# Decay rates without a logarithm, weights staged in idle buffer slots, and the order and engines of all work as one list

## The chip, the cores and the metric

One core of a Trainium2 chip runs the whole program. The time is the device time of one execution in microseconds (us), and the median of several executions is quoted. The profile covers one execution; its span, from the first to the last instruction, is 1.8 us shorter than the time of the same execution (1.77 to 1.88 in the thirteen profiled runs whose time is on record). TensorE does the matmuls, VectorE and ScalarE work on vectors (ScalarE has the table functions), GpSimd does simple vector work, and SyncE issues transfers.

## The reference, cut to what matters

```python
# 4 x 5824 tokens, 256 channels
log_a = 8 * sigmoid(r_gate) * log(clip(sigmoid(a_param)))   # decay per token and channel
a_t   = exp(log_a)
x_g   = sqrt(max(1 - a_t * a_t, 1e-6)) * sigmoid(i_gate) * x
h     = a_t[:, t] * h + x_g[:, t]        # a recurrence over the 5824 tokens
# then, token by token, with w1, w2 (256 x 1024), w3 (1024 x 1024), w_out (1024 x 256)
out   = ((h @ w1) * (h @ w2)) @ w3 @ w_out
```

The kernel computes w3 @ w_out once, at the start (the "fold"), so that each token needs two up products and one down product.

## The kernel before

The 23296 tokens are 46 chunks: one of 256 and 45 of 512. For each chunk c: load r, i and x; tanh of r and i on ScalarE; turn to channel-major, on TensorE for the first chunks and by a transfer for the rest; decay (an exp on ScalarE, scaled by the decay rate `la4`); square, root, gate, scan; cast of the state to bf16 (y); up products `pa` and `pb` in four parts mp; copy of `pa` from PSUM (the memory that TensorE writes to) to SBUF (the working memory) as `sa`; product `g_t = sa * pb` on VectorE; down product `po`; eviction; store. What the argument touches:

```python
def rates():                                   # from a_param to the decay rate
    nc.scalar.activation(out=la4, in_=la4, func=AF.Exp, scale=-1.0)
    nc.scalar.activation(out=la4, in_=la4, func=AF.Ln, bias=1.0)
    nc.vector.tensor_scalar(la4, la4, -1.0, LN_LO, op0=ALU.mult, op1=ALU.max)
    nc.vector.tensor_scalar(la4, la4, LN_HI, 4.0, op0=ALU.min, op1=ALU.mult)

def load_w(key, piece):                        # 14 weight pieces of 512 KB
    T[key] = held.tile([P, NCB, CT], F32, name="wf", tag="wf", bufs=NWF)   # NWF = 2
    nc.sync.dma_start(out=..., in_=piece)      # cut

def copy(c, mp):
    sa = ffn.tile([P, 2, CT], BF16, name="sa", tag="sa")
    copy_to((c, mp) in DV_COPY, sa[:, :, :w], T["pa", c, mp][:, :, :w])    # VectorE or ScalarE

def product(c, mp):
    nc.vector.tensor_mul(out=T["g", c][...], in0=T["sa", c, mp][...], in1=T["pb", c, mp][...])   # cut

DV_COPY = {(0, 1)}; DV_EVAC = {9}; DV_SQUARE = {2, 3, 10, 13}
W_CAST = {"w1": "POOL", "w2": "POOL", "wo": "POOL", "w3": "POOL"}
# ... a list scheduler with due times, offsets per kind of work and 470 single moves
#     works out the order of all instructions when the kernel is built (cut)
```

In these traces each engine runs its own instructions in the order of the program. That matters for everything below: a late operand or a long instruction holds up all that stands behind it on the same engine (at 368 to 378 us, shown below, a copy stands behind six pieces of scans and TensorE waits 1.26 us for it).

## Time and profile before

| | before |
|---|---|
| median of 3 runs | 528.69 us (525.78 to 528.93) |
| span of the profiled run | 526.2 us |
| TensorE, VectorE, ScalarE, GpSimd busy | 498.7, 433.9, 456.0, 342.6 us |
| first up product, first down product | 23.58, 64.32 us |
| decay rates ready | 10.45 us |

To read the start I use one number throughout, the **TensorE time lost** at a point: the time at which a down product starts, less the useful matmul time that stands before it in TensorE's program (each matmul at its undisturbed spacing, the warm-up matmuls at nothing). It only uses start times, and it shows where time is lost: where the number rises. The prediction reads the same thing by hand. Before the change it is 28.1 us at the first down product, of which 21.4 lie before the first up product, and 32.7 at the last: 4.6 are lost in the long middle. Two lines of the stretches (window, length, then busy us and count of TensorE, weight loads, VectorE, ScalarE, GpSimd, then granted clock, DMA share, GB/s) stand for that middle:

```profile
100.00:200.00 100.00, 97.72 (x610) 58.70 (x609) 89.70 (x76) 90.36 (x108) 68.30 (x52) 1.00 1.09 285
...
300.00:400.00 100.00, 100.00 (x619) 60.36 (x617) 87.39 (x70) 94.17 (x111) 75.74 (x57) 1.00 0.97 254
```

From 100 to 400 us (the stretch in between is in the prediction) VectorE has 10 to 14 us free in each 100, ScalarE 5 to 10. And TensorE's timeline (start, duration, engine, line, operation, tiles, count) dates the first down product:

```profile
64.32 1.91 PE L399 MATMUL po<-wp_sb,g_t 128*128 128x256 bf16 x16
```

### The profile page before, as it was taken

Reading aid. Unit: us, or ns where it says so; the run is one execution under the profiler, and the core shown is the slowest. Engines: PE = TensorE matmul, PEld = TensorE weight load, DVE = VectorE, ACT = ScalarE, POOL = GpSimd, SP = SyncE. Lnnn points to the kernel's source line nnn. Section 1 sums busy time; section 2 is a strip of 40 time slices with the busy share of each in tenths; the row PEclk is TensorE's granted clock in tenths of the full one; section 3 lists DMA queues with packets and bytes.
Section 4 is the critical chain, followed back from the end, with each engine's and each line's share of the span. In section 5 each row is a group of like instructions: output and inputs, shape, how many; then the busy total and the mean of one; then the engine's idle time right before and its main releaser. Section 6 shows DMA issues by size and latency. Waiting matters only on the chain.

```text
span 526.2 us, 8784 instructions
## 1 busy us (share of the span) xinstructions
PE 498.7 (95%) x3204; PEld 306.8 (58%) x3204; DVE 433.9 (82%) x376; ACT 456.0 (87%) x535; POOL 342.6 (65%) x270
## 2 busy tenths in 40 slices
PE   1589999999999999999999999999999999999997
PEld 0456666655555656555566565565665665656555
DVE  1799788998899979987888889898878988698842
ACT  5999898999898889989989989998999998965453
POOL 3478966785828768855886968878587667392100
PEclk9999999999999999999999999999999999999999
DMA  8989999999999998988897999968999875533113
GB/s 302 395 279 338 268 262 274 296 295 236 278 320 243 266 322 189 265 220 222 223 257 216 258 331 253 264 195 222 277 232 271 239 185 157 161 83 87 53 40 102
DMA packets 174604, 123.28 MB, mean 234 GB/s; under 512 B 84448, under 2 KB 170208, under 8 KB 174560
## 3 DMA queue, kind: packets, MB, share of 16 engines
q1 hardware_dynamic: 174288, 122.71, 84.9%
q8 instruction: 25, 0.41, 0.3%
q14 instruction: 19, 0.16, 0.1%
q10 hardware_dynamic: 272, 0.00, 0.0%
HBM read 78.91 MB, written 23.86 MB: 195 GB/s over the span
## 4 chain that ended last, share of the span: by engine, by line
PE 79%; DMA 9%; ACT 3%; DVE 3%; POOL 3%; issue 2%; SPq 0%; ACTq 0%; DVEq 0%; POOLq 0%
PE po L399 27%; PE pa L368 26%; PE pb L368 25%; DMA wf<-in_moe_w_dram 5%; DMA wf<-in_moe_w_out_dram 1%; ACT sa L376 1%; DVE h_t L349 1%; DVE g_t L388 1%; DMA rt<-th_r 1%; POOL w_t L436 1%; DMA r_t<-in_r_gate_dram 1%; POOL w_sb L436 1%; PE ptr L286 1%; PE pw L464 0%; POOL wo_sb L436 0%
## 5 line engine op out<-in xcount | busy, mean ns | idle before, releaser
L388 DVE TENSOR_TENSOR g_t<-sa,pb 128x1024 bf16<-128x1024 bf16 (+1 forms) x184 | 219.7, 1201 | 64.0 <-ACT sa L376 44.6
L368 PEld LDWEIGHTS <-w_sb 128*128 128x128 bf16 x1472 | 143.6, 98 | 141.9 <-issue 5.5
L376 ACT CAST sa<-pa 128x1024 bf16<-128x1024 f32 (+1 forms) x183 | 181.7, 1002 | 36.0 <-PE pa L368 35.1
L368 PE MATMUL pb<-y_t,w_sb 128*128 128x512 bf16 (+1 forms) x736 | 186.8, 377 | 1.3 <-DVE g_t L388 0.6
L368 PE MATMUL pa<-y_t,w_sb 128*128 128x512 bf16 (+1 forms) x736 | 186.4, 377 | 1.6 <-DVE g_t L388 1.3
L399 PE MATMUL po<-wp_sb,g_t 128*128 128x256 bf16 x1456 | 181.5, 273 | 0.0
L399 PEld LDWEIGHTS <-g_t 128*128 128x128 bf16 x1456 | 142.4, 98 | 45.9
L349 DVE TENSOR_TENSOR_SCAN h_t<-a_t,h_t,nrm 128x512 f32<-128x512 f32 (+3 forms) x90 | 132.0, 1481 | 0.7
L278 POOL TENSOR_TENSOR u_t<-th_i,x_t 128x512 bf16<-128x512 f32 x78 | 113.9, 1476 | 2.1 <-DMA x_t<-in_x_dram 1.7
L314 POOL TENSOR_TENSOR nrm<-a_t 128x512 f32<-128x512 f32 (+1 forms) x84 | 100.7, 1213 | 10.8 <-ACT a_t L307 9.5
L357 POOL CAST y_t<-h_t 128x1024 bf16<-128x1024 f32 x40 | 50.6, 1265 | 80.7 <-DVE h_t L349 75.1
L262 POOL TENSOR_SCALAR th_i<-th_i 128x1024 f32<-128x1024 f32 x42 | 54.5, 1300 | 41.0 <-ACT th_i L257 40.9
L376 ACT COPY ot<-po 128x512 f32<-128x512 f32 (+1 forms) x89 | 51.6, 583 | 16.9 <-PE po L399 16.8
L307 ACT ACTIVATE a_t<-rt,la 128x512 f32<-128x512 bf16 x74 | 58.7, 819 | 3.2 <-DMA rt<-th_r 1.8
L334 DVE SCALAR_TENSOR_TENSOR nrm<-nrm,ut 128x1024 f32<-128x1024 f32 x39 | 52.9, 1358 | 0.3 <-DMA ut<-u_t 0.2
L257 ACT ACTIVATE th_i<-i_t 128x1024 f32<-128x1024 f32 (+1 forms) x46 | 48.3, 1053 | 0.6 <-POOL u_t L278 0.5
L323 ACT ACTIVATE nrm<-nrm 128x1024 f32<-128x1024 f32 (+1 forms) x46 | 47.6, 1056 | 0.2
L250 ACT ACTIVATE th_r<-r_t 128x1024 bf16<-128x1024 f32 x37 | 39.1, 1061 | 2.0 <-DMA r_t<-in_r_gate_dram 1.7
L286 PE MATMUL ptr<-ident,th_r 128*128 128x128 bf16 x68 | 6.1, 246 | 14.9 <-ACT th_r L248 7.6
L323 ACT ACT_TABLE_LOAD x14 | 18.0, 1283 | 0.3
L307 ACT ACTIVATE a_t<-ptr,la 128x512 f32<-128x512 bf16 (+1 forms) x18 | 12.8, 751 | 2.8 <-PE ptr L286 1.4
L286 PEld LDWEIGHTS <-th_r 128*128 128x128 bf16 x68 | 5.1, 110 | 16.5 <-ACT th_r L248 14.3
(40 smaller groups left out, 142.3 us busy)
## 6 DMA issues: line engine op xcount, KB each, us to landing
r_t<-in_r_gate_dram SPq DMA_DIRECT2D x45, 512.0 KB, 6.2
i_t<-in_i_gate_dram SPq DMA_DIRECT2D x45, 512.0 KB, 5.4
x_t<-in_x_dram SPq DMA_DIRECT2D x45, 512.0 KB, 5.0
out_dram<-ot SPq DMA_DIRECT2D x89, 256.0 KB, 3.9
wf<-in_moe_w_dram SPq DMA_DIRECT2D x12, 512.0 KB, 5.6
wf<-in_moe_w_out_dram SPq DMA_DIRECT2D x2, 512.0 KB, 7.4
ut<-u_t SPq DMA_TRANSPOSE x39, 4.7
rt<-th_r SPq DMA_TRANSPOSE x37, 5.4
```

The source lines that it names most:

```text
L262: nc.gpsimd.tensor_scalar(t, t, 1.0, 1.0, op0=ALU.add, op1=ALU.mult)
L278: nc.gpsimd.tensor_mul(out=u.rearrange("p cb j q -> p j cb q")[:, js], in0=cut(t)[:, js], in1=cut(T["x", c])[:, js])
L307: nc.scalar.activation(out=a, in_=pr, func=AF.Exp, scale=la4[:, cb:cb + 1], bias=la4[:, cb:cb + 1])
L314: eng.tensor_mul(out=T["n", c][:, cb, :w], in0=T["a", c][:, cb, :w], in1=T["a", c][:, cb, :w])
L323: nc.scalar.activation(out=T["n", c][:, :, :w], in_=T["n", c][:, :, :w], func=AF.Sqrt, scale=-1.0, bias=1.0)
L334: nc.vector.scalar_tensor_tensor(out=T["n", c][:, :, :w], in0=T["n", c][:, :, :w], scalar=1e-3, in1=T["pu", c][:, :, :w], op0=ALU.max, op1 ...
L349: nc.vector.tensor_tensor_scan(T["h", c][:, cb, lo:hi], T["a", c][:, cb, lo:hi], T["n", c][:, cb, lo:hi], init, ALU.mult, ALU.add)
L357: eng.tensor_copy(out=T["y", c][:, :, :w], in_=T["h", c][:, :, :w])
L368: nc.tensor.matmul(out=pp[:, q, :w], lhsT=w_sb[:, cb, m * P:(m + 1) * P], rhs=T["y", c][:, cb, :w], start=(cb == 0), stop=(cb == NCB - 1))
L376: nc.scalar.copy(out=dst, in_=src_ps)
L388: nc.vector.tensor_mul(out=T["g", c][:, 2 * mp:2 * mp + 2, :w], in0=T["sa", c, mp][:, :, :w], in1=T["pb", c, mp][:, :, :w])
L399: nc.tensor.matmul(out=po, lhsT=T["g", c][:, k, j * P:(j + 1) * P], rhs=wp_sb[:, k, :], start=(k == 0), stop=(k == KD - 1), skip_group_che ...
```

## The change

The intent: start TensorE's stream earlier. The decay rate is worked out with one exp (a table that tanh shares) and a polynomial for log(1+z) on VectorE. Weights are staged in slots of the `a` and `nrm` buffers that are idle at the start, instead of in two slots of their own. The early gates lead the load queue. The scheduler is gone: one list, found by a new search, fixes the order of everything, and sets name the engine of each square, cast, copy and eviction (also of the casts of y and of the fold's copies, which the cut leaves out).

```diff
-    DV_SQUARE = {2, 3, 10, 13}
-    DV_EVAC = {9}
-    DV_COPY = {(0, 1)}
-    W_CAST = {"w1": "POOL", "w2": "POOL", "wo": "POOL", "w3": "POOL"}
+    DV_SQUARE = {(0, 0), (0, 1), (1, 0), ...}          # 20 half squares (8 before)
+    DV_COPY = {(0, 3), (1, 1), ..., (33, 1), (33, 2), (36, 3), ...}    # 32 copies of sa (1 before)
+    DV_EVAC = {(0, 0), (1, 1), (2, 0), ...}            # 31 evictions (2 before)
+    W_ACT = {('w2', 0), ('w3', 1), ('w3', 2), ('w3', 3)}
+    W_DVE = {('w3', 0)}
+    STAGE = {'w1': ['a', 'a'], 'w2': ['nrm', 'nrm'], 'wo': ['a', 'nrm'], 'w3': ['a', 'nrm', ...]}
+    WARM = [30, 30, 24]                                # 84 warm-up matmuls (28 before)
 ...
-        T[key] = held.tile([P, NCB, CT], F32, name="wf", tag="wf", bufs=NWF)
+        T["wf", nm, i] = held.tile([P, NCB, CT], F32, name="wf", tag=STAGE[nm][i])
 ...
+    def rates_abs():
+        nc.vector.scalar_tensor_tensor(out=zz, in0=la4, scalar=-1.0, in1=la4, op0=ALU.mult, op1=ALU.min)
+        nc.vector.tensor_scalar(la4, la4, -4.0, 0.0, op0=ALU.mult, op1=ALU.max)
+    def rates_exp():
+        nc.scalar.activation(out=zz, in_=zz, func=AF.Exp)
     def rates():
-        nc.scalar.activation(out=la4, in_=la4, func=AF.Exp, scale=-1.0)
-        nc.scalar.activation(out=la4, in_=la4, func=AF.Ln, bias=1.0)
-        ...
+        nc.vector.tensor_scalar(zd, zz, 2.0, None, op0=ALU.add)
+        nc.vector.reciprocal(zd, zd)
+        ...                                            # 11 instructions of 128x2 here, 2 in rates_abs
+    ORDER = """
+        A0. r1 r0 i0 Lw3.0 x0 i1 A1. E R1 R0 x1 V0 V1 Lw1.1 Cw1.1 I0 A2. d0.0 d0.1 d1.0 d1.1 r2 Lw1.0 ...
+        """                                            # one word for each piece of work
```

## The prediction

> **What bounds the kernel now.** I read the page's busy shares, then the stretches, then TensorE's timeline, then the chain of waits. The span is 526.2 us.
>
> ```profile
> PE 498.7 (95%) x3204; PEld 306.8 (58%) x3204; DVE 433.9 (82%) x376; ACT 456.0 (87%) x535; POOL 342.6 (65%) x270
> ```
>
> ```profile
> 0.00:25.00 25.00, 7.43 (x58) 6.20 (x58) 10.31 (x16) 19.54 (x24) 9.53 (x14) 1.00 0.94 347
> 25.00:40.00 15.00, 12.18 (x100) 7.79 (x99) 14.38 (x17) 13.69 (x17) 10.53 (x9) 1.00 0.87 291
> ...
> 200.00:300.00 100.00, 99.96 (x617) 60.15 (x615) 85.87 (x70) 94.52 (x114) 74.90 (x59) 1.00 0.88 226
> ```
>
> The page's first part gives busy time and share; the stretches below it give the window, its length, then busy us of TensorE, weight loads, VectorE, ScalarE, GpSimd. TensorE is full from 60 us on and poorly used before 40. From 200 to 300 ScalarE is 95% busy and VectorE 86%: little spare.
>
> ```profile
> 23.58 1.01 PE L368 MATMUL pa<-y_t,w_sb 128*128 128x256 bf16 x4 [0.19 <-DVE y_t L357]
> ...
> 30.32 1.04 PE L368 MATMUL pa<-y_t,w_sb 128*128 128x512 bf16 x4
> ...
> 497.65 1.03 PE L368 MATMUL pb<-y_t,w_sb 128*128 128x512 bf16 x4
> 498.52 1.04 PE L399 MATMUL po<-wp_sb,g_t 128*128 128x256 bf16 x8
> 499.39 1.03 PE L368 MATMUL pa<-y_t,w_sb 128*128 128x512 bf16 x4
> ...
> 515.84 7.16 PE L399 MATMUL po<-wp_sb,g_t 128*128 128x256 bf16 x64
> ```
>
> TensorE's timeline: the first up product starts at 23.58, the first of chunk 1 at 30.32; late, four up matmuls or eight down matmuls take 0.87 from start to start; the last matmul ends at 523.0. That gives TensorE's floor: 1440 wide up matmuls, 360 x 0.865 = 311; 32 half-wide, 3.5; 1456 down, 182 x 0.87 = 158; 64 fold transposes and 120 gate transposes at 0.445 per eight, 10; 64 fold products, 7. Sum 490. So 523 - 490 = 33 us are lost, and 3.2 follow the last matmul. Counting the same pieces along the timeline: 2.2 us of useful work are done by 23.6 (21.4 lost), 36 by 64.4 (28.3 lost), so only about 5 are lost in the remaining 460. The loss is the start.
>
> ```profile
> 2.60 6.74 DMA wf<-in_moe_w_dram
> 9.40 1.05 POOL w_sb L436
> 10.46 8.66 DMA wf<-in_moe_w_dram
> 19.18 2.10 POOL w_sb L436
> 21.29 4.53 DMA wf<-in_moe_w_dram
> ```
>
> ```profile
> 9.24 0.17 DVE L474 TENSOR_SCALAR la<-la 128x2 f32<-128x2 f32 x1 [7.68 <-ACT la L473]
> 9.44 1.01 DVE L475 TENSOR_SCALAR la<-la 128x2 f32<-128x2 f32 x1
> ```
>
> First, the chain of waits, in order of time: 14 weight pieces go through two staging buffers, each load waiting for GpSimd's cast of an earlier one; with pieces of that chain up to 53 us. Then VectorE's timeline: the decay rates are ready only at 10.45, so the first decays start at 10.55 although their transposes ended at 8.4.
>
> **What the Trainium skill says.** "TensorE: Matmul & The Clock Gate", "Wait — 56ns, not 53.3ns?": 215.7 ns from start to start at N=512 once warm, 106.7 at N=128 cold; the trace agrees (4 in 0.865; 12 first transposes in 1.46). "ScalarE: Activation LUTs", "Table sets: the hidden batching unit": exp and tanh share a set, ln is in another, so dropping ln drops reloads; the trace has 31 loads of 1.283 us, one before ln and one back to tanh. "SBUF — State Buffer", "Who interferes with whom": VectorE instructions with two SBUF inputs contend with GpSimd for one pair of ports, the other waits; the trace has scans of 512 at 1.28 undisturbed and 1.50 in the mean. "DMA: Bandwidth & Descriptors", "Where 436 GB/s comes from" puts HBM to SBUF near 358 GB/s; the trace shows 401 to 412 from 6 to 21 us, so I take the measured rate: 1.28 us per 512 KB.
>
> **The change, part by part.**
>
> *Rates.* Two activations and two table loads (1.28 each) leave ScalarE's start; eleven 128x2 VectorE instructions enter. The undisturbed one took 0.17; I take 0.2 each, 2.2 us. la arrives at about 4.3 (issue 0.73 + 3.5), its exp is first on ScalarE, rates ready about 7.2 instead of 10.45.
>
> *Queue.* Landings at 1.28 us per 512 KB, anchored at the old fifth unit (10.7): r1 5, r0 5.8, i0 6.5, w3.0 8.1, x0 8.8, i1 10.1, x1 11.4, w1.1 12.6, r2 13.9, w1.0 15.2, w2 16.5 and 17.7, i2 19, x2 21.6, w_out 22.9 and 24.1, x3 37, the last w3 39.5, x4 42. x0 used to land at 13.9.
>
> *First up product.* Tanh until 7.4; transposes end about 8.4; four decays 7.5 to 10.2; VectorE squares, casts w3.0, multiplies until 12.8; tanh of i1 to 11.35, table load, root 0.63: 13.3. U0 stands behind 60 warm-up matmuls (cold then warm, about 8.4 to 13.1), so 13.6. Gating 0.75, two scans 1.27, cast 0.6: y0 about 16.2. First up product 16.3, before 23.6: 7.3 us earlier.
>
> *Next chunks.* Staging now borrows idle a and nrm slots: by their order in the list every slot is free before its load's turn, so the old load-cast-load chain to 58 us goes. h1 ends 19.7, y1 at 21 (before 28.9). Then TensorE has chunk 1 with folds and transposes, 11 us, less about 4 of waits: U2 stands before a1.1 and waits for x2 and i2 (25), and a1.3 waits for VectorE to free a PSUM slot. Chunk 2 starts about 35, with its folds 15 us: 50; D1 and chunk 3 follow from 50 to 58.7, when a4.0 starts. By then 40.4 us of useful work are done (chunks 0 to 2: 17.3; three quarters of 3: 5.2; four down groups 3.5; folds 10.5; transposes 3.9). Loss 18.3, against 28.3: **10.0 us gained**.
>
> *Engines.* 31 more sa copies and 29 more output evictions go from ScalarE (1.01 and 0.58 each; 0.91 and 0.48 apart) to VectorE (about 1.13 and 0.6 apart), and 12 squares from GpSimd to VectorE (0.6). Table loads rise from 31 to 40, +11.5 us on ScalarE. ScalarE: -31x0.91 - 29x0.48 + 11.5 + about 6 for folds and casts = -25 us. VectorE: +35 + 17 + 7 = about +60: 434 becomes 494 of some 515 us.
>
> **Where it ends.** TensorE's work is unchanged. If the 5 us later losses stay 5, loss is 23, the span 490 + 23 + 3.2 = 516. The three timed runs are 525.78 to 528.93 against the profile's 526.2, mean 527.8, so I add about 1: 516.8, 2.1% below that mean.
>
> **Rivals.**
> 1. *VectorE becomes the bound.* For it: from 100 to 400 us it is idle 37 us, and the new list puts 21 copies, 18 evictions and 6 squares net into about that stretch, 24 + 11 + 4 = 38. In the first 100 us of TensorE's work its list adds to 102 us of undisturbed work, plus 6 or 7 of waits for the port. Against it: fewer GpSimd squares mean fewer such waits, it idles less on ScalarE's copies (44.6 us of its waits before), and scans can run ahead in six buffers. Each us that VectorE lacks is a us of TensorE. It would make the time 520 to 525.
> 2. *The transfers hide the earlier start.* The DMA share is 0.94 to 1.03 in the first 100 us. Chunk 3 needs x3 (37) and 10 us of work behind it; if transfers run at 1.4 us per 512 KB, chunks 3 and 4 slip 3 to 4 us: about 520.
> 3. *More than the start is gained.* Spreading copies removes the pauses at 144 to 150 and 463 (1.7 us) and what little else is lost, and my waits for U2 and PSUM do not occur, since the searched list puts them where it expects no wait: 511 to 513.
> 4. *More table loads hurt ScalarE.* It loses 25 us net, so it should not; 518 at worst.
>
> **Range and chances.** The floor 490, 15 us before the first up product and 3 after the last give 508, which no list of these parts goes under. A lead of 10 is the middle; rivals 1 and 2 take up to 7, rival 3 gives up to 5. So 516.8, range 510.5 to 523.5. Two per cent below 527.8 is 517.2, close to my middle, so faster by over 2% is little better than even: 0.55; within 2% 0.43; slower 0.02, for VectorE would have to cost twice what the start gives.
>
> **What would show it.** Rates ready near 7 us and y0 near 16 show parts one to three; no idle queue between 25 and 55 us shows the staging; first down product near 50 and a4.0 near 59 show the lead. VectorE near 95% busy with TensorE still over 99% from 100 to 400 shows that it just suffices; TensorE idle there after g_t, with VectorE never idle, shows rival 1. ScalarE should fall to about 430 us. I am wrong if y0 comes after 19, if TensorE loses over 8 us past 65, or if queue landings lag my list by over 3 us at x3.

## The result, and the profile after

| | before | after |
|---|---|---|
| median | 527.55 us (525.78 to 528.93, 4 runs) | 521.04 us (520.34 to 522.94, 4 runs) |
| span of the profiled run | 526.2 | 519.1 |
| VectorE, ScalarE, GpSimd busy | 433.9, 456.0, 342.6 | 478.3, 429.7, 299.9 |
| first up, first down product | 23.58, 64.32 | 17.37, 50.70 |
| TensorE time lost at first down product, at the end | 28.1, 32.7 | 18.9, 25.6 |

The ratio is 0.9896, with a 95% interval from 0.986 to 0.9931: faster by 1.0%, clear of the noise but less than 2%. A ratio is always the mean time of one kernel's fast runs over the mean of the other's of the same rounds, with the profiled run of each left out; so it isn't quite the ratio of the medians (which is 0.9877 here).

The page of the kernel after:

```profile
span 519.1 us, 8770 instructions
...
PE 498.2 (96%) x3203; PEld 309.0 (60%) x3260; DVE 478.3 (92%) x456; ACT 429.7 (83%) x493; POOL 299.9 (58%) x251
```

VectorE gained 44.4 us of work, ScalarE lost 26.3 and GpSimd 42.7. (TensorE shows 3203 matmul records where there are 3260 weight loads: 57 are missing from this trace.) The stretches, in the columns told above:

```profile
0.00:25.00 25.00, 14.37 (x163) 12.46 (x165) 17.39 (x36) 18.95 (x24) 9.07 (x13) 1.00 0.93 348
25.00:40.00 15.00, 14.74 (x123) 9.57 (x123) 14.40 (x18) 14.94 (x19) 10.22 (x10) 1.00 1.04 411
...
100.00:200.00 100.00, 98.96 (x610) 60.00 (x621) 97.22 (x89) 90.59 (x103) 69.83 (x57) 1.00 0.97 261
200.00:300.00 100.00, 99.16 (x602) 59.66 (x611) 94.72 (x87) 91.06 (x105) 67.49 (x57) 1.00 0.95 255
300.00:400.00 100.00, 96.70 (x589) 58.39 (x599) 93.59 (x80) 83.56 (x97) 60.96 (x48) 1.00 0.87 229
```

From 25 to 40 us TensorE is now busy 14.74 of 15 (12.18 before), and transfers run at 411 GB/s (291 before): neither TensorE nor the queue has the gap of the old start there. But VectorE, which had 10 to 14 us free in each 100, has 3 to 6 left. TensorE's timeline, early:

```profile
8.84 4.86 PE L238 MATMUL warm<-ident 128*128 128x128 bf16 x60
13.53 0.83 PE L167 MATMUL ptr<-ident,u_t 128*128 128x128 bf16 x12
...
17.37 0.60 PE L246 MATMUL pa<-y_t,w_sb 128*128 128x256 bf16 x4 [1.67 <-DVE y_t L233]
...
50.70 1.91 PE L277 MATMUL po<-wp_sb,g_t 128*128 128x256 bf16 x16
```

The first down product comes 13.6 us earlier by the clock, and 9.2 earlier in time lost: the difference of 4.4 is up products and folds that used to stand before it in TensorE's order and now stand behind it. VectorE's timeline shows when the rates begin and end (the second line starts the last instruction of them):

```profile
5.67 0.16 DVE L350 SCALAR_TENSOR_TENSOR zz<-la 128x2 f32<-128x2 f32 x1 [5.67 <-DMA la<-in_a_param_dram]
...
8.07 0.17 DVE L366 TENSOR_SCALAR la<-la 128x2 f32<-128x2 f32 x1
```

The bracket says what VectorE waited for: the 1 KB load of the decay parameter, which landed at 5.67 us.

Where is time lost after the start? The time lost rises by 6.7 us from the first down product to the last, nearly all of it in eleven steps: 0.39 at 78, 0.35 at 102, 0.42 at 115, 0.44 at 124, 0.37 at 210, 0.23 at 283, 1.03 at 313, 0.22 at 369, 0.84 at 376, 1.42 at 383, 0.60 at 415. Before, the 4.6 were at 145 and 152 (1.8), 188 to 199 (1.7), 240 (0.2) and 465 (0.6). The largest, at 383, and the one before it, at 376, in TensorE's timeline (the down product that dates a step comes some us after the wait):

```profile
373.92 1.02 PE L246 MATMUL pa<-y_t,w_sb 128*128 128x512 bf16 x4 [0.63 <-DVE g_t L266]
...
378.20 1.02 PE L246 MATMUL pb<-y_t,w_sb 128*128 128x512 bf16 x4 [1.26 <-DVE sa L252]
```

And VectorE at that time:

```profile
368.01 4.29 DVE L225 TENSOR_TENSOR_SCAN h_t<-a_t,h_t,nrm 128x512 f32<-128x512 f32 x3
372.23 0.53 DVE L225 TENSOR_TENSOR_SCAN h_t<-a_t,nrm 128x192 f32<-128x192 f32 x1
...
374.92 0.87 DVE L225 TENSOR_TENSOR_SCAN h_t<-a_t,h_t,nrm 128x320 f32<-128x320 f32 x1
375.71 1.32 DVE L225 TENSOR_TENSOR_SCAN h_t<-a_t,nrm 128x192 f32<-128x192 f32 x1
376.95 1.19 DVE L252 CAST sa<-pa 128x1024 bf16<-128x1024 f32 x1
```

No line has a bracket, so VectorE never idles. TensorE's next up product needs the PSUM slot that the copy at 376.95 empties, and that copy stands behind six scan pieces of chunks 33 and 34 (a boundary between sequences lies in chunk 34, so each of its two scans is cut in two) and two products. ScalarE, which could have made the copy, has nothing to do; this is its next copy:

```profile
380.12 1.01 ACT L254 CAST sa<-pa 128x1024 bf16<-128x1024 f32 x1 [4.01 <-PE pa L246]
```

The list gave this copy to VectorE at one of the spots where VectorE was fullest. The experiments ask whether that is the whole of it.

### The profile page after: what moved, and what is told of

Same layout as the page of the kernel before. It is cut to its first block, busy times and chain, and to the rows that moved or that the text cites. A ratio compares the mean times of both kernels' runs of the same rounds, so it can differ in the third digit from the quotient of the medians.

```text
span 519.1 us, 8770 instructions
## 1 busy us (share of the span) xinstructions
PE 498.2 (96%) x3203; PEld 309.0 (60%) x3260; DVE 478.3 (92%) x456; ACT 429.7 (83%) x493; POOL 299.9 (58%) x251
## 4 chain that ended last, share of the span: by engine, by line
PE 76%; DVE 16%; issue 5%; ACT 1%; DMA 1%; POOL 0%; DVEq 0%; ACTq 0%; POOLq 0%
PE pb L246 25%; PE po L277 24%; PE pa L246 23%; DVE g_t L266 6%; DVE h_t L225 4%; DVE sa L252 1%; PE pw L342 1%; DVE nrm L210 1%; PE ptr L167 1%; DMA la<-in_a_param_dram 1%; PE warm L238 1%; DVE nrm L195 1%; DVE nrm L207 1%; PE ptw L331 1%; DVE ot L252 1%
## 5 line engine op out<-in xcount | busy, mean ns | idle before, releaser
L254 ACT CAST sa<-pa 128x1024 bf16<-128x1024 f32 (+1 forms) x152 | 149.5, 1004 | 52.4 <-PE pa L246 47.2
L246 PE MATMUL pa<-y_t,w_sb 128*128 128x512 bf16 (+1 forms) x706 | 177.5, 377 | 5.0 <-DVE g_t L266 1.8
L246 PE MATMUL pb<-y_t,w_sb 128*128 128x512 bf16 (+1 forms) x709 | 177.9, 376 | 4.5 <-DVE sa L252 1.3
L225 DVE TENSOR_TENSOR_SCAN h_t<-a_t,h_t,nrm 128x512 f32<-128x512 f32 (+3 forms) x90 | 117.5, 1331 | 1.2
L233 POOL CAST y_t<-h_t 128x1024 bf16<-128x1024 f32 x38 | 44.5, 1170 | 118.1 <-DVE h_t L225 101.6
L195 POOL TENSOR_TENSOR nrm<-a_t 128x512 f32<-128x512 f32 x72 | 85.8, 1205 | 18.2 <-ACT a_t L188 18.1
L254 ACT COPY ot<-po 128x512 f32<-128x512 f32 (+1 forms) x60 | 34.7, 578 | 17.0 <-PE po L277 16.2
L252 DVE CAST sa<-pa 128x1024 bf16<-128x1024 f32 (+1 forms) x32 | 38.3, 1197 | 5.5 <-PE pa L246 5.4
L252 DVE COPY ot<-po 128x512 f32<-128x512 f32 (+1 forms) x33 | 21.9, 665 | 4.0 <-PE po L277 4.0
L195 DVE TENSOR_TENSOR nrm<-a_t 128x512 f32<-128x512 f32 (+1 forms) x20 | 18.2, 920 | 0.9 <-ACT a_t L188 0.9
```

The source lines that it names most:

```text
L195: eng.tensor_mul(out=T["n", c][:, cb, :w], in0=T["a", c][:, cb, :w], in1=T["a", c][:, cb, :w])
L225: nc.vector.tensor_tensor_scan(T["h", c][:, cb, lo:hi], T["a", c][:, cb, lo:hi], T["n", c][:, cb, lo:hi], init, ALU.mult, ALU.add)
L246: nc.tensor.matmul(out=pp[:, q, :w], lhsT=w_sb[:, cb, m * P:(m + 1) * P], rhs=T["y", c][:, cb, :w], start=(cb == 0), stop=(cb == NCB - 1))
L252: nc.vector.tensor_copy(out=dst, in_=src_ps)
L254: nc.scalar.copy(out=dst, in_=src_ps)
```

## The experiments

Twelve kernels ran, in three groups. Each was timed in five rounds beside the kernel before, whose medians were 527.35, 527.49 and 526.05 us in the three groups, so ratios are the safer measure across groups. All gave right results. TensorE time lost, in us:

| kernel | median | ratio, 95% interval | lost at first down | lost at the end |
|---|---|---|---|---|
| before | 527.55 | | 28.1 | 32.7 |
| after | 521.04 | 0.9896 [0.986, 0.9931] | 18.9 | 25.6 |
| after_again | 521.37 | 0.9886 [0.9853, 0.9919] | 18.1 | 26.3 |
| rates_old | 524.64 | 0.9945 [0.9912, 0.9978] | 21.2 | 28.1 |
| two_staging | 532.11 | 1.008 [1.0049, 1.0111] | 26.7 | 35.3 |
| before_rates | 527.02 | 0.9976 [0.9941, 1.0012] | 26.5 | 31.6 |
| copy33 | 520.09 | 0.9859 [0.9828, 0.9891] | 18.8 | 24.3 |
| late_act | 521.57 | 0.9883 [0.9855, 0.9911] | 18.9 | 27.0 |
| copies_act | 539.99 | 1.0229 [1.02, 1.0258] | 18.0 | 44.8 |
| no_warm | 526.39 | 0.9966 [0.9934, 0.9997] | 19.4 | 28.8 |
| dve_plus | 525.86 | 0.9993 [0.9965, 1.0021] | 19.0 | 30.9 |
| act_plus | 522.72 | 0.9941 [0.9912, 0.997] | 18.5 | 27.4 |
| pool_plus | 523.16 | 0.9944 [0.991, 0.9978] | 18.2 | 27.6 |
| la_first | 520.30 | 0.9891 [0.9864, 0.9919] | 18.4 | 24.8 |

### after_again: the changed kernel, unedited

> The changed kernel itself again, as the control of this group on the same chip. Every theory expects 521 us, a ratio to the kernel before of 0.987 to 0.991, the first down product near 50.7 us with about 19 us of TensorE time lost by then, and 6 to 7 us more lost after it.

521.37 us (521.04 to 523.68), a second time inside the range and 1.1% below before. Its time lost differs from the first profile's by 0.8 at the first down product and 0.7 at the end, with opposite signs, though it is the same program: differences below about 1 us between two single profiles are within what two runs of one program show.

### rates_old: the changed kernel with the old exp and logarithm

```diff
 def rates():
-    (rates_abs, rates_exp, rates: thirteen 128x2 instructions on VectorE and one exp; cut)
+    nc.scalar.preload_act_table_set("natural_log_exp_and_others")
+    nc.scalar.activation(out=la4, in_=la4, func=AF.Exp, scale=-1.0)
+    nc.scalar.activation(out=la4, in_=la4, func=AF.Ln, bias=1.0)
+    (two tensor_scalar, as before)
```

> The changed kernel with the old rates: exp, then ln from the other table set, after the tanh of i0. Theory (the rates lie on the path to the first chunk): rates ready near 9.5 us instead of 8.2, one reload more before the tanh of i1, so the root and the first up product come 2 to 2.5 us later (19.5 us) and the first down product and the end too: 523 to 523.5 us. Rival (the landing and casting of w2, which ended near 20.5 us, holds chunk 0 anyway): the first up product is later, but the first down product moves by less than 1 us, 521 to 522 us.

524.64 us, 3.3 more than after_again and more than expected. Four of its six runs had a granted clock of 0.993 to 0.997; the two at 0.999 and 1.0 took 523.81 and 523.48, 2.1 to 2.4 more than after_again. In its profile VectorE ends the rates later, and TensorE starts the first up product later, by 2.7 us than after's 17.37:

```profile
9.72 0.17 DVE L360 TENSOR_SCALAR la<-la 128x2 f32<-128x2 f32 x1
```

```profile
20.09 0.60 PE L246 MATMUL pa<-y_t,w_sb 128*128 128x256 bf16 x4 [2.09 <-DVE y_t L233]
```

The time lost is 2.3 more at the first down product and 2.5 more at the end. So in the changed kernel the rates are on the path that sets the end, and the slip stays to the end nearly unchanged. Its late steps are the same as after's to within 0.01 us (1.04, 0.85, 1.41 and 0.61, each 2.5 us later): they belong to the list, not to the timing of the start.

### before_rates: the kernel before with the new rates alone

```diff
+    rates_abs()                  # ahead of everything
     for key in rest:
+        if key == ("tanh_r", 1):
+            rates_exp()
 # the three functions as in the changed kernel; cut
```

> The kernel before with the new rates alone (exp ahead of the second tanh, polynomial on VectorE), its order kept. Theory (its start is bound by the chain of weight loads and casts): decays start near 8.5 us instead of 10.55, but the first up product and the first down product (64.5 us) move by less than 1.5 us and the time falls by 0 to 1.5 us. Rival (the rates are the path): first up product 2.5 us earlier and 2.5 to 3.5 us off the time.

527.02 us, ratio 0.9976 with an interval that includes 1. The first up product came at 22.82 instead of 23.58, and the time lost at the first down product fell by 1.6, of which 1.1 were left at the end. The same part that is worth 2.5 us in the new kernel by the time lost (3.3 by the medians) is worth about 1 in the old (0.3 by the medians). There the next thing to be waited for is close behind, as TensorE's timeline shows:

```profile
15.38 0.61 PE L288 MATMUL ptr<-ident,u_t 128*128 128x128 bf16 x4 [3.19 <-DVE u_t L275]
```

TensorE waits for the first u product, which needs x, and x doesn't lead the queue in that kernel.

### two_staging: the changed kernel with two staging buffers of its own

```diff
-        T["wf", nm, i] = held.tile([P, NCB, CT], F32, name="wf", tag=STAGE[nm][i])
+        T["wf", nm, i] = held.tile([P, NCB, CT], F32, name="wf", tag="wf", bufs=2)
 # and in the list each later weight load moved behind the cast that frees its slot
```

> The changed kernel with the old staging: all 14 weight pieces go through two buffers of their own, and each load stands in the queue right behind the cast that frees its buffer. Theory (staging in idle slots is most of the early gain): loads wait for casts again and hold up the gate loads behind them; the first down product comes at 56 us or later instead of 50.7 and the time is 526 to 529 us, nearly all of the gain gone. Rival (transfers were bound by bandwidth, the buffers do not matter): below 2 us, 521 to 523 us.

532.11 us: 10.7 more than after_again and slower than before, more than I expected. The time lost is 26.7 at the first down product, 7.8 more than after's, and 1.9 more is lost later. TensorE's granted clock was 0.93 in the first 25 us and 0.89 from 25 to 40 (1.0 in after), and transfers ran at 284 and 320 GB/s there (348 and 411). Waits of the load queue in the first 80 us (what waits, what it waited for, us, times, longest):

```profile
SPq L317 <- DMA wf<-in_moe_w_dram: 9.9, 7, 2.4
SPq L317 <- ACT w_t L324: 5.3, 3, 3.3
...
SPq L317 <- POOL wo_sb L326: 2.8, 2, 1.6
SPq L317 <- POOL w_sb L326: 2.6, 3, 1.4
```

The queue is in order, so while a weight load waits for a cast, the gates behind it wait too: the i gate of chunk 2 is issued at 14.56, at 8.84 in after. The staging is what makes the rest of the new start possible. How much of the 10.7 a list searched for two buffers would win back was not tried, and what the lower clock adds was not separated.

### no_warm: the changed kernel without its warm-up matmuls

```diff
-        ... Lw2.1 W1 I1 s0.0 ... s1.1 W0 U0 ... y0 W2 a0.2 ...
+        ... Lw2.1 I1 s0.0 ... s1.1 U0 ... y0 a0.2 ...
```

> The changed kernel without its 84 warm-up matmuls. The transposes of chunk 0's u, now behind 60 of them (13.5 us), can start at 10.9; the first gating waited 0.8 us for them. Theory (the warm-ups buy a fast clock for the first up products, which else run at half speed for 3 to 4 us): first up product 0.5 us earlier, first down product 1 to 2 us later, 522 to 523 us. Rival (chunk 0 waits for weights and y1 anyway, the warm-ups are in the way): 520.5 to 521 us.

526.39 us, 5.0 more than after_again, and more than expected. The first up product came earlier than in after, but cold, at half speed (the granted clock on record is 1.0 in the first 25 us all the same):

```profile
16.02 1.01 PE L246 MATMUL pa<-y_t,w_sb 128*128 128x256 bf16 x4 [1.78 <-DVE y_t L233]
...
18.59 1.92 PE L246 MATMUL pa<-y_t,w_sb 128*128 128x256 bf16 x8
```

Four matmuls take 1.01 us where after's take 0.60. At the first down product only 0.5 us more is lost than in after; the rest comes later, as steps of 1.56 at 117, 1.14 at 208 and 0.80 at 233, where after has 0.4, 0.4 and none. The profiled run, at 524.70, is one of the faster of its six, 3.3 more than after_again's. At the first and the third of these steps scans on VectorE last longer beside GpSimd's work (1.78 and 1.91 us where after's take 1.28 and 1.27; 2.11 where 1.33); before the second, ScalarE waits 2.48 us for the load of a gate where it waits 1.19 in after. That the missing warm-ups bring this about is not shown: the first step stands in late_act too (below), with all its warm-ups.

### copy33: two copies back to ScalarE at the largest late loss

```diff
     DV_COPY = {...
-        (33, 1), (33, 2),
         ...}
```

> The changed kernel with only the two sa copies of chunk 33 moved from VectorE back to ScalarE. In the changed kernel TensorE waited there for one of them (378.2 us, 1.26 us) and lost 2.3 us between 369 and 384, behind six scan pieces on VectorE, while ScalarE was idle for 4.0 us. Theory (VectorE's list is too full there): these 2.3 us shrink to under 1, time 519.3 to 520.2 us. Rival (the chunk boundary's scans hold y back whoever copies): less than 0.5 us changes, or the loss comes back at the next chunk.

520.09 us (519.57 to 521.21), ratio 0.9859. The step of 1.42 at 383 is gone and no other grew: 24.3 lost at the end, 1.3 less than after. Of what was lost between 369 and 384, 1.1 us is left, where the theory said under 1. On VectorE the products now follow the scan piece at once, with no copy between them:

```profile
375.77 1.32 DVE L223 TENSOR_TENSOR_SCAN h_t<-a_t,nrm 128x192 f32<-128x192 f32 x1
377.01 2.32 DVE L264 TENSOR_TENSOR g_t<-sa,pb 128x1024 bf16<-128x1024 bf16 x2
```

```profile
376.84 1.03 PE L244 MATMUL pb<-y_t,w_sb 128*128 128x512 bf16 x4
```

TensorE's line has no bracket where it waited 1.26 us before. Two words of the list were on the wrong engine. This version beats both kernels by its median, though its interval overlaps that of the changed kernel; only one of its six runs is above the fastest of after_again's six, on the same chip.

### late_act: all copies and evictions of chunks 33 and later back to ScalarE

```diff
-    DV_COPY = {..., (33, 1), (33, 2), (36, 3), (40, 2), (41, 2), (41, 3), (44, 0), (45, 0)}
+    DV_COPY = {...}          # no entry of a chunk of 33 or more
-    DV_EVAC = {..., (33, 1), (34, 1), (35, 0), (35, 1), (41, 1), (42, 0), (42, 1)}
+    DV_EVAC = {...}
```

> The changed kernel with all sa copies and output evictions of chunks 33 to 45 moved from VectorE back to ScalarE (8 copies, 7 evictions). Theory (VectorE too full, ScalarE with spare time: 80% in that stretch): the losses of 2.3 us near 376 and 0.6 us near 415 go, time 518.5 to 519.7 us. Rival (ScalarE's reloads need the room): new waits of TensorE for ScalarE's copies eat it, 521 to 523 us.

521.57 us: no change, as the rival had it, though it contains copy33's edit. The step at 383 is gone, but new ones appear: 1.36 at 425, 0.69 at 469, 0.45 at 507, and 1.53 instead of 0.42 at 116, where the two lists are alike (so that one is a run's own variation). The timelines of VectorE and GpSimd show what makes it, first in after, then in late_act:

```profile
109.49 1.27 DVE L225 TENSOR_TENSOR_SCAN h_t<-a_t,h_t,nrm 128x512 f32<-128x512 f32 x1
109.62 3.43 POOL L160 TENSOR_TENSOR u_t<-th_i,x_t 128x512 bf16<-128x512 f32 x2 [0.53 <-DMA ut<-u_t]
```

```profile
109.47 2.38 DVE L221 TENSOR_TENSOR_SCAN h_t<-a_t,h_t,nrm 128x512 f32<-128x512 f32 x1
109.50 3.40 POOL L156 TENSOR_TENSOR u_t<-th_i,x_t 128x512 bf16<-128x512 f32 x2 [0.43 <-DMA ut<-u_t]
```

The same scan lasts 1.1 us longer when GpSimd's products begin 0.03 us behind it instead of 0.13, and the copy that TensorE needs stands behind the scan. In its waits from 340 us on, TensorE now waits for ScalarE's copies (1.3 us in three waits) where it waited for VectorE's. Moving single copies at a spot where they hurt helps; moving a class of them moves the loss.

### copies_act: all 26 copies of chunks 8 and later back to ScalarE

```diff
-    DV_COPY = {...32 entries...}
+    DV_COPY = {(2, 1), (1, 1), (0, 3), (7, 2), (3, 2), (1, 3)}
```

> The changed kernel with all 26 sa copies of chunks 8 to 45 moved from VectorE back to ScalarE (the evictions stay). Theory (VectorE without spare time is the reason for the 6.7 us lost after the first down product): loss after 53 us falls to 3 to 5 us, time 517.5 to 519.5 us. Rival (ScalarE with 39 reloads cannot carry them; the move was needed): ScalarE is over 95% busy from 100 to 300 us, TensorE waits for its copies, time 522 to 528 us.

539.99 us, 18.6 more than after_again, at a granted clock of 0.994. This went against what I put first, that the moves to VectorE had cost as much as they gave, and lies beyond the rival's 522 to 528, too. The stretch and the waits from 100 to 340 us:

```profile
200.00:300.00 100.00, 92.41 (x545) 53.93 (x543) 79.79 (x71) 87.36 (x100) 57.95 (x48) 0.97 0.82 225
```

```profile
DVE g_t L264 <- ACT sa L252: 22.1, 10, 4.7
...
PE pa L244 <- ACT sa L252: 6.6, 6, 2.3
PE pb L244 <- ACT sa L252: 3.0, 2, 2.7
```

ScalarE is the culprit at 87 to 91% busy (the rival had said over 95), and VectorE idles 22.1 us for its copies. ScalarE itself idles 17.5 us in this window, before copies whose `pa` TensorE has not yet made. A busy share near 90% doesn't say that an engine has room: its work is in a fixed order, so that it is late for one engine while it waits for another. How far a list searched for this assignment would repair it was not tried, so the 18.6 us are the cost of the move within this list.

### dve_plus, act_plus, pool_plus: 25 extra instructions on one engine

```diff
+    def more(c, mp):
+        if 8 <= c < 33 and mp == 1:
+            nc.vector.memset(junk, 0.0)            # dve_plus: behind product(c, 1)
+            nc.scalar.copy(out=junk, in_=junk_i)   # act_plus: behind copy(c, 1)
+            nc.gpsimd.tensor_copy(out=junk, in_=junk_i)   # pool_plus: behind product(c, 1)
```

(One of the three lines in each kernel; the two tiles and the memset that fills `junk_i` at the start are cut.) This measures what a microsecond of each engine is worth in the middle of the changed kernel.

> The changed kernel with one more instruction on VectorE for each of chunks 8 to 32: a memset of a 128x512 tile that nothing reads, behind a product; 25 in all, some 0.3 to 0.6 us each, 8 to 15 us of added work. Results stay right. Theory (VectorE has no time to spare between 100 and 340 us: it is busy 97, 95 and 94% there, and it moved from 434 to 478 us of work): most of it comes out of TensorE's time, so 3 to 10 us longer than the changed kernel's 521.4, 524.5 to 531.5, and more than the two sisters with the same work on ScalarE and on GpSimd. Rival (what TensorE loses late is lost at a few spots of the list and not for want of capacity): under 2 us longer, and like the sisters.

> The same with a copy of a 128x512 tile on ScalarE behind a copy of the same chunk: 25 in all, about 0.5 us each, 13 us added. ScalarE is busy about 91% from 100 to 300 us, so it has some 20 us to spare there. Theory (VectorE is the engine without spare time): 0 to 3 us longer than the changed kernel, 521 to 524.5, clearly less than the VectorE sister. Rival: every delay behind which TensorE's data stands costs alike, whatever the engine's busy share: as long as the VectorE sister or longer.

> The same with a copy of a 128x512 tile on GpSimd: 25 in all, about 0.6 us each, 15 us added. GpSimd is busy 68% from 100 to 300 us. Theory: 0 to 2 us longer, 521 to 523.5, through the port that it shares with VectorE at most 4. Rival (the shared port makes GpSimd's work VectorE's own): as long as the VectorE sister.

The extra instruction took 0.485 us on VectorE (12.1 in all), 0.628 at the median on ScalarE (15.7) and 0.609 at the median on GpSimd (15.2; some waited, so the sum is 19.1). Between about 125 us and the end the time lost rose by 10.2, 7.2 and 8.2 us, where after's and la_first's rise by 5.1. So the added work cost 5.1, 2.1 and 3.1 us of TensorE's time: 42% of it on VectorE, 13% on ScalarE, 20% on GpSimd (each from one profile, so to about 1 us; the order of the last two isn't settled). One step of pool_plus, 1.40 at 440, stands in after_again as well (1.41 at 439), where nothing was added; without it GpSimd's share is 1.7 us, 11%. The times agree with that: 525.86, 522.72 and 523.16 are 5.6, 2.4 and 2.9 over la_first, which ran on the same chip in the same rounds and equals the changed kernel in ratio. The stretches and waits of dve_plus:

```profile
100.00:200.00 100.00, 98.61 (x615) 59.16 (x614) 97.94 (x95) 89.49 (x102) 67.99 (x57) 1.00 0.95 257
200.00:300.00 100.00, 97.25 (x590) 57.34 (x588) 97.55 (x95) 88.46 (x102) 64.94 (x54) 1.00 0.92 249
```

```profile
PE pb L250 <- DVE g_t L270: 3.1, 5, 1.0
PE pa L250 <- DVE g_t L270: 2.6, 6, 0.6
PE pb L250 <- DVE sa L256: 1.1, 1, 1.1
```

VectorE is 98% busy, and TensorE's waits for it (from 66 us on) rise from 3.4 to 6.8 us. The theory held: VectorE is the engine with the least to spare. But it isn't TensorE's equal as a bound: more than half of the added work still found gaps, and the loss stands in separate steps and not as a slow drift. The Trainium skill says in "SBUF — State Buffer", section "Who interferes with whom", that VectorE and GpSimd lock each other out of a shared port pair. The lines under late_act agree with it (one scan at 1.27 or 2.38 us beside GpSimd's products). That GpSimd's share here comes from it is not shown: in pool_plus VectorE's busy time is 482.5 us, 4.2 more than in after, but no_warm's is 481.3 with no work added.

### la_first: the small load first

```diff
-    nc.scalar.dma_start(out=la4, in_=a_param.rearrange("(cb p) -> p cb", p=P))
+    nc.sync.dma_start(out=la4, in_=a_param.rearrange("(cb p) -> p cb", p=P))
```

> The changed kernel with the 1 KB load of the decay parameter issued first on SyncE's queue, ahead of the early gates, and not on ScalarE's queue beside them, where it landed at 5.67 us. Theory (its late landing, 1.4 us behind what was predicted, is why the rates came at 8.24 and not at about 7.2, and why the first up product came at 17.4 and not at 16.3): it lands 1 us or more earlier, the rates are ready at 6.7 to 7.6, the first up product starts 0.5 to 1.2 us earlier, and the time falls by 0 to 1 us, to 520.3 to 521.5. Rival (the gates, which are now issued some 0.4 us later, or the u products set the first up product): rates earlier, first up product at 17.2 to 17.8 and the time as before or up to 0.5 longer.

The decay parameter landed at 2.89 us instead of 5.67 (2.1 us from issue instead of 4.9), the rates were ready at 5.47 instead of 8.24, and the first up product came at 16.25 instead of 17.37, or 16.96 in after_again. VectorE and TensorE:

```profile
2.89 0.16 DVE L350 SCALAR_TENSOR_TENSOR zz<-la 128x2 f32<-128x2 f32 x1 [2.89 <-DMA la<-in_a_param_dram]
...
5.30 0.17 DVE L366 TENSOR_SCALAR la<-la 128x2 f32<-128x2 f32 x1
8.55 0.42 DVE L195 TENSOR_TENSOR nrm<-a_t 128x256 f32<-128x256 f32 x1 [3.08 <-ACT a_t L188]
```

```profile
16.25 0.60 PE L246 MATMUL pa<-y_t,w_sb 128*128 128x256 bf16 x4 [1.10 <-DVE y_t L233]
```

The rates came 2.8 us earlier, but the first square only 0.4 (8.55 for 8.94): the rates had left the path, and VectorE now waits 3.08 us for the first decays, which stand behind the tanh of an i gate for which ScalarE waits until 7.43. The gating of chunk 0 starts at 13.57, for 14.03 in after and 13.67 in after_again. The rest of the gain at the first up product is not the rates': the two scans and the cast behind the gating took 1.40 and 0.43 us here, 2.07 and 0.43 in after, 1.27 and 1.17 in after_again, which is the same program as after. Of the 0.7 to 1.1 us at the first up product nothing certain is left at the first down product (18.4 lost, between 18.1 and 18.9). The median of 520.30 lies at the lower end of what was expected, and the ratio of 0.9891 is that of the changed kernel. Both sides of the expectation are half right: the first up product moved as the theory said, though mostly for another reason, and the late landing costs nothing that this measurement can see.

## Why the prediction was right or wrong

The time of 521.04 us lies within the range, and the change was faster, by 1.0%; but the middle was 4.2 us too low, and "faster by over 2%", to which I gave 0.55, did not occur; what came is "within 2%", at 0.43. By its own steps:

- **What bounds the kernel, and the floor: right.** 490 + 25.6 + 3.2 gives 518.8 for a span of 519.1; before, 490 + 32.7 + 3.2 gives 525.9 for 526.2.
- **Rates: the mechanism right, one term off.** They were said to be ready at "about 7.2" and were at 8.24. The polynomial was sized well (2.57 us from landing to end with its exp); the landing of `la` was not: 5.67 for 4.3. la_first shows it, since the same load lands 2.1 us after issue when nothing is ahead of it. rates_old shows that the new rates are worth 2.5 us in this kernel by the time lost, 3.3 by the medians.
- **Queue, and the staging: right.** Transfers moved 411 GB/s from 25 to 40 us, x3 landed at 38.2 for 37, and rival 2 didn't occur: neither VectorE nor ScalarE waits for a transfer from 20 to 60 us. two_staging shows that the staging carries it (10.7 us).
- **First up product: 17.37 for 16.3.** The gating started at 14.03 for 13.6, after u transposes that stood behind the warm-up matmuls; the larger part is in the two scans, put at 1.27 and measured at 2.07 (1.27 in after_again). "Next chunks" had two errors that nearly cancelled: GpSimd cast y1 from 22.30 to 23.33, behind a weight, where I had 21; but the "about 4 of waits" on U2 and a PSUM slot hardly occurred (0.8 us of TensorE's waits from 24 to 51).
- **The lead: right.** "10.0 us gained" was 9.2 at the first down product.
- **Engines: right in direction.** ScalarE 429.7 (predicted about 430), table loads 31 to 40 as counted. VectorE 478.3 instead of 494: +44 where I had +60. Most of the difference stands in the two pages: 90 of the 98 pieces of scans took 1.33 us each instead of 1.48, 13.5 us less in all. Why was not tested; fewer waits for the port, with GpSimd 42.7 us less busy, would fit.
- **"If the 5 us later losses stay 5": the step that failed.** They became 6.7 (6.4 in la_first, 8.2 in after_again, where the prediction's limit for being wrong was 8). And it is not the 4.6 of before that stayed: the old steps from 145 to 465 are gone, and new ones came, the four largest (3.9 us in all) from 313 to 415, at waits for VectorE's products and copies.
- **Rival 1, in part.** I had it as "each us that VectorE lacks is a us of TensorE", giving 520 to 525. The time is in that span, TensorE's waits do name VectorE, and the sign I set ("TensorE idle there after g_t, with VectorE never idle") is what the trace shows at 368 to 378. But the price is 0.42 us per us, not 1, and copies_act shows that the moves to VectorE were needed by this list. So VectorE is not the bound; it has become the engine whose delays reach TensorE first. Of rival 3, what it named came true (the old pauses are gone, its waits hardly occurred), but the new steps outweigh it; rival 4 did not occur (from 66 us on TensorE's listed waits, 3.4 us, are all for VectorE).
- **From the span to the run.** I added "about 1" (0.8 in the sum) where every run shows 1.8.

The sum, from 516.8: 2.6 for the loss (25.6 for 23: 0.6 by the first down product, 1.7 after it, 0.3 because 18.3 and 5 were rounded to 23), 1.0 for the step from span to run, 0.5 because the pieces of the floor don't quite close and I rounded 516.2 to 516, and 0.2 because the profiled run lay below the median: 4.3 for 4.2, rounding included. So the failed step is the largest single term, but less than half of the miss.

no_warm, late_act and after_again lose up to 1.5 us at spots where after, with the same list there, loses 0.4 or nothing. In all of them but one (no_warm's gate load) the traces show VectorE instructions that last longer beside GpSimd's work: the scans told above, and in after_again a cast at 433.0 of 1.53 us that takes 0.69 in after, with GpSimd's work begun 0.8 us before the cast in the one and 0.01 behind it in the other. What stays open is how a list can be made that does not depend on such tenths of a us.

## What to carry to other kernels

When the start of a kernel is shortened, its gain in TensorE time need not survive to the end, if work is moved to pay for it (here 2.1 of 9.2 us were lost again in the long middle): count the lost time at several points, not only at the start and the end. What a part is worth depends on what stands right behind it (the new rates: 2.5 us in the new kernel, about 1 or less in the old), so measure it by taking it out of the new kernel as well as by putting it alone into the old. Price an engine by adding known work to it, and look for the few spots where TensorE waits while another engine idles: moving two copies there won about 1 us, moving twenty-six lost 19.

## What the Trainium skill lacked or had wrong

- "DMA: Bandwidth & Descriptors", section "Where 436 GB/s comes from", says that about 358 GB/s binds for HBM to SBUF. This kernel, with its one core, moved 411 GB/s from 25 to 40 us. "HBM Reference", section "Specifications (TRN2)", has it right (about 425 GB/s for a core that streams alone); the first section should say so.
- "ScalarE: Activation LUTs", section "What ACT_TABLE_LOAD costs", puts a switch of table sets at about 1.283 us for the load and 1.38 for a drain, 2.66 in all. The load is so here (1.283 us, the mean of the 20 loads ahead of the roots), but no drain is to be seen: a root ends at 14.53, the load starts at 14.55, the next activation at 15.84.
- No page that I read says what a tiny load costs beside a busy queue. "DMA: Bandwidth & Descriptors", section "Queues, rings and completion order", says that an engine takes turns between queues packet by packet; the 1 KB load on ScalarE's queue took 4.9 us beside loads of 512 and 256 KB that SyncE issued at 0.74 and 1.19, and 2.1 when it was issued first.
- No page that I read gives a way to price an engine that is nearly full. Here 12.1 us of added work on a VectorE that was 95 to 97% busy cost 5.1 us, 15.7 us on a ScalarE at 91% cost 2.1, and ScalarE failed at 87% (18.6 us) when it had more copies than its list was made for.
